# Loading the keys of a decode attention in 64 KB runs, on five slots used from both ends in turn

## The chip, the cores and the metric

The kernel runs on one core of one Trainium2 chip. The metric is the device time of one execution in microseconds (us). The profile is one execution of the same program under the hardware profiler. Its span begins with the first instruction of the program and is about 1.8 us shorter than the time.

## The reference

One new token for a batch of two passes two branches which a gate mixes: a small MLP mixer, and attention over a long cache. Only the attention matters here, because it reads nearly all the bytes.

```python
B, Sq, D = 2, 1, 1024
H, Sk, Dh = 32, 16384, 128          # k_cache, v_cache: (B, H, Sk, Dh) in bfloat16, 268 MB each
q = (x @ wq).reshape(B, Sq, H, Dh).transpose(0, 2, 1, 3)
scores = einsum("bhqd,bhkd->bhqk", q, k_cache) * Dh ** -0.5
p = softmax(scores, axis=-1)
o = einsum("bhqk,bhkd->bhqd", p, v_cache)
a = o.transpose(0, 2, 1, 3).reshape(B, Sq, H * Dh) @ wo
out = g * a + (1 - g) * b           # b: the MLP branch, g: a sigmoid gate
```

## The kernel before

The 64 pairs of batch and head are processed in 32 *couples* of two heads. A partition holds 256 consecutive positions of one head, which are 64 KB in one run in HBM. In the on-chip memory a ring of four slots of 32 KB per partition takes all large loads. The values of a couple take slots 0 and 1 in one load. The keys come as two loads of one slot each, so in runs of 32 KB.

```python
NRS = 4
SLOT = J * Dh                                    # 32 KB a partition
k_slots = (3, 2)
def q_k(n):                                      # keys of couple n: two loads
    for t in range(2):
        queue_load(("k", n, t), [lambda e, idx, t=t: e.dma_start(ring[:, idx, :],
                   kv_src(A_k, n)[:, t * SLOT:(t + 1) * SLOT])], (k_slots[t],))
def q_v(n):                                      # values of couple n: one load
    queue_load(("v", n), [lambda e, idx: e.dma_start(ring[:, idx:idx + 2, :].rearrange("p s m -> p (s m)"),
                                                     kv_src(A_v, n))], (0, 1))
# ... cut: all loads are queued in the order K0 V0 K1 V1 ..., and each is issued, in this order,
#     by the sync engine as soon as the last reader of its slots has signalled.

for n in range(NPR):                             # 32 couples; a hardware loop on TensorE, VectorE, ScalarE
    ev_z = do_Z(n)
    for c in range(NU // TC):                    # 8 chunks, 4 to a slot
        ev_t = do_T(n, c)                        # VectorE transposes a chunk of keys in place
        for t in range(TC):
            do_S(n, c * TC + t, ...)             # TensorE: scores; the slot is released after its 4th chunk
    ev_pt, ev_rc = do_softmax(n)
    ev_OT = do_out(n, do_PV(n, ev_pt), ev_rc)    # TensorE: probabilities times values; releases slots 0 and 1
# ... cut: at the end do_aproj multiplies with Wo, which comes in one load of 4 MB and six smaller pieces.
```

Of the kernel before, what the change touches and what calls it, by code (L numbers as in the profile page):

```python
# [7 lines left out]
ALU = mybir.AluOpType  # L8
AX = mybir.AxisListType
BF16 = mybir.dt.bfloat16  # L10
F32 = mybir.dt.float32
# [109 lines left out]
def build_kernel(nc, A_x, A_k, A_v, A_wq, A_wo, B_w1, B_w2, B_w3, B_w4, gate_w, out, dbg=None):  # L121
    dbg = dbg or {}
    B, Sq, D = A_x.shape
    _, H, Sk, Dh = A_k.shape
# [3 lines left out]
    P = 128  # L128
    J = Sk // P
    assert J == P  # L130
    HP = 2
    NU = 16
    JU = HP * J // NU
    UH = NU // HP
    NBP = 4
    G = B * H
    NPR = G // HP
    assert H % HP == 0
    NBD = D // P
    NBF = F // P  # L140
    NRS = 4
    SLOT = J * Dh
    NCOL = JU * 32
    ZO = 2 * (NU - 1)
# [17 lines left out]
    with ExitStack() as st:  # L162
        block = st.enter_context(nc.Block())
        sb = lambda name, shape, dt: st.enter_context(nc.sbuf_tensor(name, shape, dt))
        ring = sb("ring", [P, NRS, SLOT], BF16)
        ident = sb("ident", [P, P], BF16)
# [24 lines left out]
        recip = sb("recip", [P, HP], F32)  # L191
        OT_sb = sb("OT_sb", [P, G], BF16)
        rA = sb("rA", [P, 1], F32)
        hsel = sb("hsel", [P, HP, P], F32)
        gTt = sb("gTt", [P, NPR // B, B], F32)
        OT4_sb = sb("OT4_sb", [P, R4, NCT, 2], BF16)
        xrow = sb("xrow", [P, DQ], BF16)
        bgrow = sb("bgrow", [P, DQ], F32)
# [17 lines left out]
        gT = sb("gT", [P, 4], F32)  # L216
# [3 lines left out]
        esems = {e: sem("e_" + e) for e in ENGS}  # L220
        s_ring = [sem(f"dr{i}") for i in range(NRS)]
        s_misc = sem("dmisc")
# [4 lines left out]
        pl = _Plan(esems)  # L227
# [33 lines left out]
        for hp in range(HP):  # L261
# [7 lines left out]
                    waits=(ev_rowm,), sig=True)  # L269
# [3 lines left out]
                        waits=(e0,), sig=True)  # L273
# [3 lines left out]
        slot_of = {}  # L277
        slots_of = {}
        slot_free = {i: () for i in range(NRS)}

# [6 lines left out]
        def queue_load(key, fns, slots):  # L287
            dma_q.append((key, fns, slots))
# [9 lines left out]
                    dma_done[key] = dma_done[key, k] = pl.dma("sp", (lambda e, fn=fn, idx=slots[0]: fn(e, idx)), dsem,  # L298
                                                              waits=waits if k == 0 else ())

        def release(key, ev):
            for idx in slots_of[key]:
                assert idx not in slot_free
                slot_free[idx] = tuple(ev) if isinstance(ev, (tuple, list)) else (ev,)
            pump()

        def arrived(key):
            assert key in dma_done, f"load {key} not yet issued in program order (would deadlock)"
            return dma_done[key]
# [17 lines left out]
        wloads = {}  # L327
# [20 lines left out]



        w_slots = [0, 1, 2, 3, 0, 1, 2]
        k_slots = (3, 2)
        n_w = [0]

        def q_load(key):
# [3 lines left out]
        def kv_src(T, n):  # L359
            h, b = n // B * HP, n % B  # L360
            return T[b, h:h + HP].rearrange("h (p j) d -> (h p) (j d)", p=P // HP)

        def q_k(n):
            for t in range(2):
                queue_load(("k", n, t), [lambda e, idx, t=t: e.dma_start(ring[:, idx, :], kv_src(A_k, n)[:, t * SLOT:(t + 1) * SLOT])],
                           (k_slots[t],))

        def q_v(n):
            queue_load(("v", n), [lambda e, idx: e.dma_start(ring[:, idx:idx + 2, :].rearrange("p s m -> p (s m)"), kv_src(A_v, n))],
# [13 lines left out]
        evd = {}  # L383
# [13 lines left out]
        def rd5w():  # L397
            return (b5_lw[0],) + tuple(b5_rd)

        def rd5(ev):  # L400
            b5_rd.append(ev)
            return ev
# [5 lines left out]
        def st_gate():  # L408
            e1 = pl.add("dve", lambda e: e.tensor_tensor(zz[:, 0, :, :], xT_f[:, :, :],
                                                         gwT_f[:, :].unsqueeze(2).broadcast_to([P, NBD, 2]), op=ALU.mult),  # L410
                        waits=(evd["xT_f"], evd["gwT"]), sig=True)
            e2 = pl.add("dve", lambda e: e.tensor_reduce(gin[:, 0:2], zz[:, 0, :, :].rearrange("p n b -> p b n"), axis=AX.X, op=ALU.add),
                        waits=(e1,), sig=True)
            e3 = mm5(g_ps, ones_f[:, :], gin[:, 0:2], waits=(e2, ev_const), sig=True)
            e4 = rd5(pl.add("act", lambda e: e.activation(th[:, 0:2], g_ps, ACT.Tanh, scale=0.5), waits=(e3,) + rd5w(), sig=True))
            pl.add("dve", lambda e: e.tensor_scalar(gT[:, 0:2], th[:, 0:2], 0.5, 0.5, op0=ALU.mult, op1=ALU.add),
                   waits=(e4,), sig=True)
            evd["g"] = pl.add("dve", lambda e: e.tensor_scalar(gT[:, 2:4], th[:, 0:2], -0.5, 0.5, op0=ALU.mult, op1=ALU.add),
                              waits=(e4,), sig=True)
            evd["gTt"] = pl.add("dve", lambda e: e.tensor_copy(gTt[:, :, :], gT[:, 0:2].unsqueeze(1).broadcast_to([P, NPR // B, B])),  # L420
                                waits=(evd["g"],), sig=True)
            e5 = pl.add("dve", lambda e: e.tensor_tensor(gm[:, :], gT[:, 2:4], m2[:, :], op=ALU.mult),
                        waits=(evd["g"], ev_const), sig=True)
            evd["grow"] = pl.add("dve", lambda e: e.tensor_reduce(grow[:, :], gm[:, :], axis=AX.X, op=ALU.add), waits=(e5,), sig=True)
# [126 lines left out]
        key = ("w2", 0)  # L551
# [3 lines left out]
        for hi in range(NHI):  # L555
            key = ("w3", hi)
# [3 lines left out]
        for pi, (k0, kn) in enumerate(w4_parts):  # L560
            key = ("w4", pi)
            put([row_stage(key, list(range(c * R4, (c + 1) * R4)), k0 * R4, kn * R4, lambda kc: GT_bf[:, kc, :], "GT",
                               last=(c == kn - 1)) for c in range(kn)], key)
# [5 lines left out]
        for qd in range(NQ):  # L569
            ev_xr = pl.dma("act", lambda e, qd=qd: e.dma_start(xrow[32 * qd:32 * qd + 2, :], A_x[:, 0, qd * DQ:(qd + 1) * DQ]), s_xr,  # L570
                           waits=(ev_xr0,))
# [6 lines left out]
            q_k(n)  # L578
            q_v(n)
        for pi in range(2):  # L580
            queue_load(("wo", pi), wloads[("wo", pi)], (k_slots[pi],))
        pump()

        def xrow4(row, b_n, nb):
# [4 lines left out]
        last = None  # L589
        for nb in range(NBD):  # L590
            last = pl.add("pe", lambda e, nb=nb: e.transpose(tr_ps[:, nb * 4:nb * 4 + 2], xrow4(xg_row, 2, nb), ident[0:2, 0:2]),
                          waits=(ev_x, ev_ident), sig=(nb == NBD - 1))
# [8 lines left out]
        first = True  # L601
        ev = None
        for hi in range(NHI):
            key = ("wq", hi)
            ev_arr = arrived(key)
            wv = ring_w(slot_of[key], R4, HD)
            for r in range(R4):
                kc = hi * R4 + r
                for h in range(H):
# [4 lines left out]
                    ev = pl.add("pe", fn, waits=(ev_arr, ev_xT_bf) if h == 0 else (), sig=lastmm)  # L614
                    first = False
# [4 lines left out]
        for bp in range(NBP):  # L620
            evp = pl.add("pe", lambda e, bp=bp: e.matmul(q4_ps[:, bp, :], lhsT=PermQ[:, bp, :],  # L621
                                                        rhs=q_sb[:, :, :].rearrange("p h b -> p (h b)"), start=True, stop=True),
                         waits=(ev_q, ev_const, ev_r0), sig=(bp == NBP - 1))
# [3 lines left out]
        for nb in range(NBD):  # L627
            lastg = pl.add("pe", lambda e, nb=nb: e.transpose(gw_ps[:, nb, 0:1], xrow4(gw_row, 1, nb), ident[0:1, 0:1]),
                           waits=(ev_gw, ev_const), sig=(nb == NBD - 1))
        evd["gwT"] = pl.add("dve", lambda e: e.tensor_copy(gwT_f[:, :], gw_ps[:, :, 0]), waits=(lastg,), sig=True)  # L630
        pro_ev = (ev_q, ev_q4, evd["gwT"], evd["xT_f"], ev_xT_bf)
# [6 lines left out]
        oT_ps = banks[7][:, 0:HP]  # L638
        PH = P // HP
        TC = 2  # L640
# [10 lines left out]
                    waits=(ev_q4, ev_const, ev_S.get(n - 1)), sig=(hp == HP - 1))  # L651
            return ev

        def do_T(n, c):
            key, o = ("k", n, c * TC // UH), c * TC % UH * JU * Dh
            ap = ring[:, slot_of[key], o:o + TC * JU * Dh].bitcast(F32)
            return pl.add("dve", lambda e: e.transpose(ap, ap), waits=(arrived(key),), sig=True)  # L657

        def do_S(n, u, w):
            key, o = ("k", n, u // UH), u % UH * JU * Dh  # L660
            kv = ring[:, slot_of[key], o:o + JU * Dh].rearrange("p (j b k t) -> p j b k t", j=JU, b=2, k=32)
            end = u % UH == UH - 1
            for bp in range(NBP):
                ev = pl.add("pe", lambda e, bp=bp: e.matmul(  # L664
                    S_ps[:, 0:NCOL], lhsT=Z[:, bp, ZO - 2 * u:ZO - 2 * u + P], rhs=kv[:, :, bp // 2, :, bp % 2],
                    start=(u == 0 and bp == 0), stop=(u == NU - 1 and bp == NBP - 1), skip_group_check=True),
                    waits=w, sig=(end and bp == NBP - 1))
                w = ()
            if end:
                ev_S[n] = ev  # L670
                release(key, ev)

        def do_softmax(n):
            e1 = pl.add("dve", lambda e: e.tensor_reduce(rA[:, :], S_ps[:, 0:NCOL], axis=AX.X, op=ALU.max), waits=(ev_S[n],), sig=True)  # L674
# [33 lines left out]
        def do_out(n, ev_pv, ev_rc):  # L708
            e1 = pl.add("act", lambda e: e.activation(acc_sb[:, :], acc_ps[:, 0:512], ACT.Copy), waits=(ev_pv,), sig=True)  # L709
            for w in range(4):  # L710
                e2 = pl.add("pe", lambda e, w=w: e.matmul(oT_ps, lhsT=acc_sb[:, w * P:(w + 1) * P], rhs=dsel[:, w, :],  # L711
                                                          start=(w == 0), stop=(w == 3)), waits=(e1,) if w == 0 else (), sig=(w == 3))
            return pl.add("dve", lambda e, i: e.scalar_tensor_tensor(  # L713
                OT_sb[:, bass.ds(i * HP, HP)], oT_ps, gTt[:, :, :].rearrange("p m b -> p (m b)")[:, bass.ds(i, 1)], recip[:, :],
                op0=ALU.mult, op1=ALU.mult), waits=(e2, ev_rc), sig=True, dyn=True)

        def do_aproj():
            o4_ps = banks[7][:, 16:16 + R4 * NCT * 2].rearrange("p (r c b) -> p r c b", r=R4, b=2)
# [24 lines left out]
        for n in range(NPR):  # L743
            pl.mark[n] = {e: len(pl.ops[e]) for e in ENGS}
            ev_z = do_Z(n)
            for c in range(NU // TC):
                ev_t = do_T(n, c)
                for t in range(TC):
                    do_S(n, c * TC + t, () if t else (ev_t, ev_z) + (pro_ev if c == 0 else ()) if c == 0 else (ev_t,))
            ev_pt, ev_rc = do_softmax(n)  # L750
            ev_OT = do_out(n, do_PV(n, ev_pt), ev_rc)
        pl.mark[NPR] = {e: len(pl.ops[e]) for e in ENGS}
# [4 lines left out]
        for b, eng in enumerate(("sp", "act")):  # L757
            ev_out = pl.dma(eng, lambda e, b=b: e.dma_start(out[b, 0, :].rearrange("(q n) -> q n", q=NQ), orow[b:PR:32, :]), s_out[b],
                            waits=(ev_fin,))
            pl.add(eng, lambda e, ev=ev_out: e.wait_ge(ev.sem, ev.val))  # L760

        def loop_of(name):
            first = pl.mark[0][name]
            return first, pl.mark[1][name] - first, NPR

        @block.gpsimd
        def _(e):
# [64 lines left out]
```

## Time and profile before

| | before |
|---|---|
| time, median of 4 | 1329.43 us (1329.35 to 1329.55) |
| bytes read | 570.4 MB |
| packets of the load queue | 17,000 |
| from couple to couple (landings of values) | 38.780 us |
| last value landing, last Wo landing | 1304.43, 1324.41 us |

A packet is one run of bytes that one of the 16 DMA engines moves (or the 4 bytes with which it reports a load's end; they take their engine 6 ns in the packet records of before). The last row comes from the trace's landing records: a load leaves 16 records there, one for each DMA engine, and has landed with the last. These lines are from the page of before. The first two rows under the span give busy time and share by engine, the DMA row is the busy share of the DMA engines in 40 slices of the span, and the last rows are groups of instructions: busy time, mean ns of one, then the engine's idle time just before them and what ended it.

```profile
span 1327.6 us, 12590 instructions
...
PE 803.9 (61%) x5306; PEld 327.0 (25%) x5306; DVE 659.3 (50%) x521; ACT 45.7 (3%) x99; POOL 20.1 (2%) x101
...
DMA  9999999999999999999999999999999999999998
...
q1 hardware_dynamic: 17000, 570.43, 99.7%
q8 instruction: 8, 0.13, 0.0%
...
DMA 72%; DVE 16%; PE 6%; issue 6%; SPq 0%; ACT 0%
...
L657 DVE STREAM_TRANSPOSE ring<-ring 128x2048 f32<-128x2048 f32 x256 | 569.0, 2280 | 108.6 <-DMA ring<-in_A_k_cache_dram 108.6
...
L700 PE MATMUL ps<-ring,PT_sb 128*32 128x512 bf16 x2048 | 183.4, 537 | 152.7 <-DMA ring<-in_A_v_cache_dram 152.7
```

No compute engine is busy for more than 61% of the span, but the load queue q1 fills 99.7% of the 16 engines' time, and the DMA row stands at 90% or more in every slice but the last. Both the transposes of keys and the matmuls on values start when a DMA lands. q8: the 8 packets of 16 KB there are blocks of instructions.

One couple in the timeline of before (start, duration, engine, line, operation; in brackets the idle time before it and what ended it; SPq is the sync engine issuing a load):

```profile
606.43 6.00 PE L700 MATMUL ps<-ring,PT_sb 128*32 128x512 bf16 x64 [4.55 <-DMA ring<-in_A_v_cache_dram]
...
612.48 0.33 SPq L369 DMA_DIRECT2D ring<-in_A_v_cache_dram  x1
...
616.12 8.89 DVE L657 STREAM_TRANSPOSE ring<-ring 128x2048 f32<-128x2048 f32 x4 [2.26 <-DMA ring<-in_A_k_cache_dram]
...
625.84 8.89 DVE L657 STREAM_TRANSPOSE ring<-ring 128x2048 f32<-128x2048 f32 x4 [0.83 <-DMA ring<-in_A_k_cache_dram]
627.16 9.90 SPq L365 DMA_DIRECT2D ring<-in_A_k_cache_dram  x2
```

The first half of the keys lands at 616.1 us and the second at 625.8. The next keys are issued at 627.2, while the values are in flight until 645: every load is queued long before its predecessor ends.

### The profile page before, as it was taken

The page shows a single profiled execution, that of the slowest core. Times are in us where ns is not written, and L with a number is a line of the kernel's source. Part 1 is how long each engine was busy: PE and PEld are TensorE (multiplying, and loading weights), DVE is VectorE, ACT ScalarE, POOL GpSimd, SP SyncE. Part 2 cuts the span into 40 slices and gives each one's busy share as a digit, 9 for nine tenths or more (in the row PEclk, how much of TensorE's full clock was granted, in tenths as well). Part 3 has the DMA queues.
Part 4 walks back from the last instruction along what each step waited for, and adds up shares of the span by engine and source line. Part 5 has one row for each costly group of instructions (what it writes and reads, how often), then busy time and mean ns, then how long its engine had stood idle before and what let it go on. Part 6 is the DMA issues. An engine that isn't in the chain of part 4 may idle for free.

```text
span 1327.6 us, 12590 instructions
## 1 busy us (share of the span) xinstructions
PE 803.9 (61%) x5306; PEld 327.0 (25%) x5306; DVE 659.3 (50%) x521; ACT 45.7 (3%) x99; POOL 20.1 (2%) x101
## 2 busy tenths in 40 slices
PE   3456555766655566665557666555656655565764
PEld 3322221222222222222222222222222222222222
DVE  1065544466544456654445665444566544456650
ACT  0000000000000000000000000000000000000000
POOL 2000000000000000000000000000000000000000
PEclk9997778778877877887778787777888777788877
DMA  9999999999999999999999999999999999999998
GB/s 400 429 439 429 440 427 427 433 431 439 432 440 427 422 436 431 436 440 427 430 430 432 434 436 442 427 427 429 432 433 440 434 427 436 425 434 429 447 430 348
DMA packets 17041, 570.60 MB, mean 430 GB/s; under 512 B 1779, under 2 KB 1795, under 8 KB 2182
## 3 DMA queue, kind: packets, MB, share of 16 engines
q1 hardware_dynamic: 17000, 570.43, 99.7%
q8 instruction: 8, 0.13, 0.0%
q14 instruction: 3, 0.02, 0.0%
q10 hardware_dynamic: 30, 0.01, 0.0%
HBM read 570.44 MB, written 0.00 MB: 430 GB/s over the span
## 4 chain that ended last, share of the span: by engine, by line
DMA 72%; DVE 16%; PE 6%; issue 6%; SPq 0%; ACT 0%
DMA ring<-in_A_k_cache_dram 66%; DVE ring L657 16%; PE ps L664 5%; DMA ring<-in_B_w_dram 2%; DMA ring<-in_A_wo_dram 2%; DMA ring<-in_A_wq_dram 2%; SPq L324 0%; PE ps L514 0%; PE ps L612 0%; PE ps L485 0%; PE ps L405 0%; DVE orow L756 0%; DVE q_f L624 0%; PE ps L734 0%; PE ps L621 0%
## 5 line engine op out<-in xcount | busy, mean ns | idle before, releaser
L664 PE MATMUL ps<-ring,Z 128*128 128x512 bf16 x2048 | 540.0, 418 | 217.8 <-DVE ring L657 217.3
L657 DVE STREAM_TRANSPOSE ring<-ring 128x2048 f32<-128x2048 f32 x256 | 569.0, 2280 | 108.6 <-DMA ring<-in_A_k_cache_dram 108.6
L664 PEld LDWEIGHTS ps<-ring,Z 128*128 128x128 bf16 x2048 | 199.9, 104 | 545.1 <-issue 273.4
L700 PE MATMUL ps<-ring,PT_sb 128*32 128x512 bf16 x2048 | 183.4, 537 | 152.7 <-DMA ring<-in_A_v_cache_dram 152.7
L713 DVE SCALAR_TENSOR_TENSOR OT_sb<-ps,gTt,recip 128x2 f32 x32 | 7.0, 219 | 368.3 <-PE ps L711 368.3
L700 PEld LDWEIGHTS ps<-ring,PT_sb 128*32 128x32 bf16 x2048 | 67.6, 130 | 255.4 <-DMA ring<-in_A_v_cache_dram 155.4
L674 DVE TENSOR_REDUCE rA<-ps 128x1 f32<-128x512 f32 x32 | 22.1, 691 | 64.3 <-PE ps L664 64.3
L685 ACT ACTIVATE P_sb<-ps,negm 128x512 bf16<-128x512 f32 x32 | 22.0, 687 | 851.5 <-DVE negm L683 851.5
L689 PE MATMUL ps<-rowsum,hsel 128*128 128x1 f32 x128 | 23.8, 290 | 37.9 <-ACT P_sb L685 37.9
L687 DVE STREAM_TRANSPOSE PT_sb<-P_sb 128x512 bf16<-128x512 bf16 x32 | 22.8, 711 | 27.0 <-ACT P_sb L685 27.0
L709 ACT ACTIVATE acc_sb<-ps 128x512 bf16<-128x512 f32 x32 | 19.1, 597 | 363.4 <-PE ps L700 363.4
L689 PEld LDWEIGHTS ps<-rowsum,hsel 128*128 128x128 f32 x128 | 21.1, 234 | 40.7 <-ACT P_sb L685 40.7
L647 POOL TENSOR_TENSOR Z<-q_f,mask 128x8 bf16<-128x8 f32 x64 | 12.3, 226 | 1208.2 <-PE ps L664 1208.2
L676 PE MATMUL ps<-ident,rmax_bf 128*1 128x128 bf16 x32 | 7.0, 217 | 33.1 <-DVE rmax_bf L675 33.1
L711 PE MATMUL ps<-dsel,acc_sb 128*128 128x2 bf16 x128 | 8.1, 167 | 22.7 <-ACT acc_sb L709 22.7
L612 PE MATMUL ps<-xT_bf,ring 128*128 128x2 bf16 x256 | 7.1, 165 | 17.8 <-DMA ring<-in_A_wq_dram 17.8
L711 PEld LDWEIGHTS ps<-dsel,acc_sb 128*128 128x128 bf16 x128 | 5.3, 96 | 38.4 <-ACT acc_sb L709 38.4
L676 PEld LDWEIGHTS ps<-ident,rmax_bf 128*1 128x1 bf16 x32 | 2.5, 79 | 49.1 <-DVE rmax_bf L675 49.1
L677 DVE TENSOR_REDUCE m_sb<-ps 1x2 bf16<-1x128 bf16 x32 | 8.9, 279 | 9.9 <-PE ps L676 9.9
L683 DVE TENSOR_SCALAR negm<-ps,cAB 128x1 f32<-128x1 f32 x32 | 8.8, 276 | 9.2 <-PE ps L680 9.2
L680 PE MATMUL ps<-m_sb,ones_bf 1*64 1x1 bf16 x64 | 6.1, 186 | 11.9 <-DVE m_sb L677 11.9
L514 PE MATMUL ps<-ring,GT_bf 128*2 128x256 bf16 x112 | 6.3, 415 | 10.1 <-DMA ring<-in_B_w_dram 10.1
(93 smaller groups left out, 91.0 us busy)
## 6 DMA issues: line engine op xcount, KB each, us to landing
ring<-in_A_k_cache_dram SPq DMA_DIRECT2D x64, 4096.0 KB, 27.8
ring<-in_A_wq_dram SPq DMA_DIRECT2D x2, 4096.0 KB, 17.5
ring<-in_B_w_dram SPq DMA_DIRECT2D x2, 3584.0 KB, 32.3
ring<-in_B_w_dram SPq DMA_DIRECT2D x1, 4096.0 KB, 28.5
ring<-in_A_wo_dram SPq DMA_DIRECT2D x1, 4096.0 KB, 26.5
ring<-in_B_w_dram SPq DMA_DIRECT2D x1, 3072.0 KB, 29.1
ring<-in_A_wo_dram SPq DMA_DIRECT2D x3, 1024.0 KB, 23.0
ring<-in_B_w_dram SPq DMA_DIRECT2D x1, 2048.0 KB, 27.3
```

The source lines that it names most:

```text
L647: ev = pl.add("pool", lambda e, hp=hp: e.tensor_tensor(Z[:, :, ZO:ZO + P].rearrange("p t (i c) -> p t i c", c=32)[:, :, 2 * hp:2 * hp + 2, ...
L657: return pl.add("dve", lambda e: e.transpose(ap, ap), waits=(arrived(key),), sig=True)
L664: ev = pl.add("pe", lambda e, bp=bp: e.matmul(S_ps[:, 0:NCOL], lhsT=Z[:, bp, ZO - 2 * u:ZO - 2 * u + P], rhs=kv[:, :, bp // 2, :, bp % 2], ...
L674: e1 = pl.add("dve", lambda e: e.tensor_reduce(rA[:, :], S_ps[:, 0:NCOL], axis=AX.X, op=ALU.max), waits=(ev_S[n],), sig=True)
L676: e3 = pl.add("pe", lambda e: e.transpose(mt_ps, rmax_bf[:, :], ident[:, :]), waits=(e2,), sig=True)
L677: e4 = pl.add("dve", lambda e: e.tensor_reduce(m_sb[0:1, :], mt_ps.rearrange("o (h p) -> o h p", h=HP), axis=AX.X, op=ALU.max), waits=(e3, ...
L685: e7 = pl.add("act", lambda e: e.activation(P_sb[:, :], S_ps[:, 0:NCOL], ACT.Exp, bias=negm[:, 0:1], scale=scale, accum_out=rowsum[:, 0:1] ...
L687: e8 = pl.add("dve", lambda e: e.transpose(PT_sb[:, :], P_sb[:, :]), waits=(e7,), sig=True)
L689: e9 = pl.add("pe", lambda e, hp=hp: e.matmul(l_ps[:, hp:hp + 1], lhsT=hsel[:, hp, :], rhs=rowsum[:, 0:1], start=True, stop=True, skip_gro ...
L700: ev = pl.add("pe", lambda e, jj=jj, cg=cg: e.matmul(acc_ps[32 * cg:32 * cg + 32, 0:512], lhsT=PT_sb[:, 32 * jj:32 * jj + 32], rhs=vv[:, 4 ...
L709: e1 = pl.add("act", lambda e: e.activation(acc_sb[:, :], acc_ps[:, 0:512], ACT.Copy), waits=(ev_pv,), sig=True)
L711: e2 = pl.add("pe", lambda e, w=w: e.matmul(oT_ps, lhsT=acc_sb[:, w * P:(w + 1) * P], rhs=dsel[:, w, :], start=(w == 0), stop=(w == 3)), w ...
```

## The change

Keys are to come in 64 KB runs as the values do, one load a couple. A fifth slot would not hold a second pair, so couples take turns: even ones lie in slots 3 and 4 and are processed from the lower half, odd ones in slots 2 and 3, from the upper half. In either case slot 3 is processed first, and its release together with the slot that is free already lets the next keys be issued. The hardware loop now spans two couples and runs 16 rounds.

```diff
-    NRS = 4
+    NRS = 5
 ...
-        w_slots = [0, 1, 2, 3, 0, 1, 2]
-        k_slots = (3, 2)
+        w_slots = [0, 1, 2, 3, 4, 0, 1]
+        k_slots = ((3, 4), (2, 3))
+        k_order = ((0, 1), (1, 0))
 ...
-            for t in range(2):
-                queue_load(("k", n, t), [lambda e, idx, t=t: e.dma_start(ring[:, idx, :], kv_src(A_k, n)[:, t * SLOT:(t + 1) * SLOT])],
-                           (k_slots[t],))
+            queue_load(("k", n), [lambda e, idx: e.dma_start(ring[:, idx:idx + 2, :].rearrange("p s m -> p (s m)"), kv_src(A_k, n))],
+                       k_slots[n % 2])
 ...  (do_T, do_S: take their chunk from the two slots; do_S releases one slot of the two after each half;
 ...   a small table gTt gives way to the gate itself, now that the batch index is fixed within the loop body)
-            queue_load(("wo", pi), wloads[("wo", pi)], (k_slots[pi],))
+            queue_load(("wo", pi), wloads[("wo", pi)], ((4, 3)[pi],))
 ...
-            for c in range(NU // TC):
-                ev_t = do_T(n, c)
+            us = [h * UH + v for h in k_order[n % 2] for v in range(UH)]
+            for k in range(0, NU, TC):
+                ev_t = do_T(n, us[k])
 ...
-            return first, pl.mark[1][name] - first, NPR
+            return first, pl.mark[2][name] - first, NPR // 2
```

More of the change, by code (lines that the diff above doesn't have):

```diff
@@ L194, in build_kernel @@
         hsel = sb("hsel", [P, HP, P], F32)
-        gTt = sb("gTt", [P, NPR // B, B], F32)
         OT4_sb = sb("OT4_sb", [P, R4, NCT, 2], BF16)
@@ L299, in pump, with release @@
                                                               waits=waits if k == 0 else ())
-        def release(key, ev):
-            for idx in slots_of[key]:
+        def release(key, ev, slots=None):
+            for idx in slots or slots_of[key]:
                 assert idx not in slot_free
@@ L419, in st_gate @@
                               waits=(e4,), sig=True)
-            evd["gTt"] = pl.add("dve", lambda e: e.tensor_copy(gTt[:, :, :], gT[:, 0:2].unsqueeze(1).broadcast_to([P, NPR // B, B])),
-                                waits=(evd["g"],), sig=True)
             e5 = pl.add("dve", lambda e: e.tensor_tensor(gm[:, :], gT[:, 2:4], m2[:, :], op=ALU.mult),
@@ L652, in do_Z, with chunk, do_T, do_S @@
             return ev
-        def do_T(n, c):
-            key, o = ("k", n, c * TC // UH), c * TC % UH * JU * Dh
-            ap = ring[:, slot_of[key], o:o + TC * JU * Dh].bitcast(F32)
-            return pl.add("dve", lambda e: e.transpose(ap, ap), waits=(arrived(key),), sig=True)
-        def do_S(n, u, w):
-            key, o = ("k", n, u // UH), u % UH * JU * Dh
-            kv = ring[:, slot_of[key], o:o + JU * Dh].rearrange("p (j b k t) -> p j b k t", j=JU, b=2, k=32)
+        def chunk(n, u, nu):
+            o = u * JU * Dh
+            return ring[:, slot_of["k", n]:slot_of["k", n] + 2, :].rearrange("p s m -> p (s m)")[:, o:o + nu * JU * Dh]
+        def do_T(n, u):
+            ap = chunk(n, u, TC).bitcast(F32)
+            return pl.add("dve", lambda e: e.transpose(ap, ap), waits=(arrived(("k", n)),), sig=True)
+        def do_S(n, u, w, first, last):
+            kv = chunk(n, u, 1).rearrange("p (j b k t) -> p j b k t", j=JU, b=2, k=32)
             end = u % UH == UH - 1
@@ L665, in do_S @@
                     S_ps[:, 0:NCOL], lhsT=Z[:, bp, ZO - 2 * u:ZO - 2 * u + P], rhs=kv[:, :, bp // 2, :, bp % 2],
-                    start=(u == 0 and bp == 0), stop=(u == NU - 1 and bp == NBP - 1), skip_group_check=True),
+                    start=(first and bp == 0), stop=(last and bp == NBP - 1), skip_group_check=True),
                     waits=w, sig=(end and bp == NBP - 1))
@@ L670, in do_S @@
                 ev_S[n] = ev
-                release(key, ev)
+                release(("k", n), ev, (slots_of["k", n][u // UH],))
         def do_softmax(n):
@@ L712, in do_out @@
                                                           start=(w == 0), stop=(w == 3)), waits=(e1,) if w == 0 else (), sig=(w == 3))
+            b = n % B
             return pl.add("dve", lambda e, i: e.scalar_tensor_tensor(
-                OT_sb[:, bass.ds(i * HP, HP)], oT_ps, gTt[:, :, :].rearrange("p m b -> p (m b)")[:, bass.ds(i, 1)], recip[:, :],
-                op0=ALU.mult, op1=ALU.mult), waits=(e2, ev_rc), sig=True, dyn=True)
+                OT_sb[:, bass.ds(i * B * HP + b * HP, HP)], oT_ps, gT[:, b:b + 1], recip[:, :], op0=ALU.mult, op1=ALU.mult),
+                waits=(e2, ev_rc), sig=True, dyn=True)
         def do_aproj():
@@ L745, in build_kernel @@
             ev_z = do_Z(n)
-            for c in range(NU // TC):
-                ev_t = do_T(n, c)
+            us = [h * UH + v for h in k_order[n % 2] for v in range(UH)]
+            for k in range(0, NU, TC):
+                ev_t = do_T(n, us[k])
                 for t in range(TC):
-                    do_S(n, c * TC + t, () if t else (ev_t, ev_z) + (pro_ev if c == 0 else ()) if c == 0 else (ev_t,))
+                    w = () if t else (ev_t,) if k else (ev_t, ev_z) + pro_ev
+                    do_S(n, us[k + t], w, k + t == 0, k + t == NU - 1)
             ev_pt, ev_rc = do_softmax(n)
```

## The prediction

> **What bounds the kernel now.** The DMA engines. The page gives 570.6 MB in 1327.6 us, with the load queue's packets filling 99.7% of the 16 engines' span. By the packet records the engines idle about 5.5 us in the mean, 3.7 us of it behind the last weight load. In the chain of waits the DMA has 72%; the DVE transposes in it (16%) only stand there because a key load's issue waits for its slot, far ahead of need. Landings of couples are 38.78 us apart: two key loads of 4 MB at 9.712 us each, a value load of 8 MB at 19.354 us: 16.78 MB at 432.7 GB/s. [...]
>
> **What the change removes.** Keys come in 64 KB runs, as values do. A 64 KB packet takes its engine 2.419 us, a 32 KB packet about 1.214 us, so joining two saves some 9 ns; one completion descriptor (6 ns) per load and engine goes too. By landings: 2 x 9.712 - 19.354 = 0.070 us a couple, x 32 = 2.2 us, all on the critical path, as the queue is never empty. The gTt copy was not critical.
>
> **What it adds and moves.** Work on keys begins only when all 8 MB have landed, one half (9.7 us) later. With T this landing:
> - The first half is scored about T + 12 (now 10.95 to 12.6 us from landing to the issue its release allows); then the next keys are issued. The fastest engines finish the values ahead of them about T + 17.5: margin 5 us; from an issue to its first packet passes about 1 us.
> - The second half follows without pause (eight transposes of 2.27 us, 18 us); softmax is done near T + 23.5 (14.6 us from a half's landing to transposed probabilities). Values landed at T + 19.4, so PV now waits 4 us for softmax, not for the DMA. It takes 5 to 6 us; the next values are issued near T + 30, the queue runs dry only at T + 37: margin 7 us.
> - Prologue: the first values still wait for the last W4 matmuls (66.7 us), with keys in flight until about 81.
> - Tail: Wo loads are issued no later than needed; the last PV ends about 4 us later, near the landing of the first Wo load, and its last pieces still come after. Ending unchanged.
> - The loop body doubles, 16 rounds. Instruction loads are 8 packets of 16 KB in the whole run; I expect no more inside the loop.
>
> So 1329.5 - 2.2 = **1327.3 us**, eight times in ten between 1326.4 and 1328.4. Faster by over 2%: 1%. Within 2%: 96%. Slower by over 2%: 3%.
>
> **What would show it.** Landings of couples 38.71 us apart; the load queue's 17,000 packets fewer by some 4,600, key packets 64 KB at 2.42 us; engine idle not over 6 us; the wait ahead of PV's first matmul ends with the transposed probabilities, not the values; DVE waits for keys once a couple, 10 to 15 us.
>
> **What would make it wrong.** An issue too late: were the TensorE clock halved (now 7 to 10 us after each pause) over a whole first half, scoring it would take 16 us and the key margin fall to 1 us; starvation would show as engine idle time once a couple. Or instruction reloads in the longer loop that burden one DMA engine.

For the 16 us at half clock: in the trace of before the granted clock falls to 0.5 in 65 stretches, 63 of which last 6.8 or 10.2 us (601.0 to 611.3 and 614.7 to 621.5 us in the couple above). In the second of them a matmul on keys came every 0.43 us, so 32 of them and the first transpose would take 16 us, by estimate.

## The result, and the profile after

The changed kernel takes 1328.49 us (median of 4, 1328.13 to 1328.50) against 1329.43 us. The ratio is 0.9992 with a 95% interval of 0.9975 to 1.0009. A ratio here is the mean time of one kernel's fast runs over that of the other's fast runs of the same rounds, so not quite the ratio of the medians quoted. By this interval alone the two are the same; the eight single times do not overlap, however, and the trace shows where the 0.9 us comes from.

The page of after:

```profile
span 1326.7 us, 12413 instructions
...
PE 778.5 (59%) x5306; PEld 329.5 (25%) x5306; DVE 655.4 (49%) x520; ACT 45.7 (3%) x99; POOL 20.1 (2%) x101
...
DMA  9999999999999999999999999999999999999998
...
q1 hardware_dynamic: 12392, 570.43, 99.6%
q8 instruction: 9, 0.15, 0.0%
...
DMA 71%; PE 22%; DVE 6%; SPq 1%; issue 0%
...
L658 DVE STREAM_TRANSPOSE ring<-ring 128x2048 f32<-128x2048 f32 x256 | 565.2, 2275 | 278.6 <-DMA ring<-in_A_k_cache_dram 278.6
...
L700 PE MATMUL ps<-ring,PT_sb 128*32 128x512 bf16 x2048 | 169.6, 505 | 4.5 <-DVE recip L691 4.5
```

The same bytes come in 4,608 packets fewer. The matmuls on values (L700) no longer wait for a DMA: the idle time before them fell from 152.7 to 4.5 us, as softmax is now what comes last. In the chain of waits the DMA keeps its 71%; that TensorE's matmuls now stand there for the transposes means only that they release the slot for the next keys, far ahead of need. One couple in the timeline of after:

```profile
586.12 17.66 DVE L658 STREAM_TRANSPOSE ring<-ring 128x2048 f32<-128x2048 f32 x8 [8.50 <-DMA ring<-in_A_k_cache_dram]
...
597.20 0.33 SPq L365 DMA_DIRECT2D ring<-in_A_k_cache_dram  x1
...
609.68 6.50 PE L700 MATMUL ps<-ring,PT_sb 128*32 128x512 bf16 x64
...
616.24 0.33 SPq L369 DMA_DIRECT2D ring<-in_A_v_cache_dram  x1
```

All eight transposes run without a pause from the landing at T = 586.1. The next keys are issued at T + 11.1, the matmuls on values start at T + 23.6, and the next values are issued at T + 30.1. The queue still never runs dry: over all couples, keys are issued at least 4.8 us before the fastest engine has finished the load ahead of them, and values at least 6.3 us.

The landing records of the two traces, us from the start of the span:

| | before | after | gained so far |
|---|---|---|---|
| values of the first couple | 102.27 | 102.33 | -0.06 |
| values of the last couple | 1304.43 | 1302.07 | 2.36 |
| last Wo piece but one | 1323.76 | 1321.44 | 2.32 |
| last Wo piece | 1324.41 | 1323.51 | 0.90 |
| end of the span | 1327.61 | 1326.68 | 0.93 |

So the couples gained what was expected: (1304.43 - 102.27) / 31 = 38.780 us each before, 38.701 after, 0.078 us a couple. But 1.4 us was given back in the last of 78 landings. The end of before:

```profile
1321.87 1.02 PE L734 MATMUL ps<-ring,OT_sb 128*2 128x256 bf16 x16 [1.87 <-DMA ring<-in_A_wo_dram]
1323.14 1.04 PE L734 MATMUL ps<-ring,OT_sb 128*2 128x256 bf16 x12 [0.25 <-DMA ring<-in_A_wo_dram]
1324.45 0.38 PE L734 MATMUL ps<-ring,OT_sb 128*2 128x256 bf16 x4 [0.27 <-DMA ring<-in_A_wo_dram]
```

and of after:

```profile
1320.79 0.39 PE L735 MATMUL ps<-ring,OT_sb 128*2 128x256 bf16 x8 [0.65 <-DMA ring<-in_A_wo_dram]
1321.49 0.28 PE L735 MATMUL ps<-ring,OT_sb 128*2 128x256 bf16 x4 [0.30 <-DMA ring<-in_A_wo_dram]
1323.55 0.28 PE L735 MATMUL ps<-ring,OT_sb 128*2 128x256 bf16 x4 [1.78 <-DMA ring<-in_A_wo_dram]
```

The last four matmuls waited 1.78 us for their piece of Wo where before they waited 0.27. In the packet records one of the 16 engines pauses in after from 1320.97 to 1322.04 us, with seven packets of 2 KB of that last piece to go: the time of a q8 packet of 16 KB, 1320.97 to 1322.05. This is a block of TensorE's instructions: u_pad7 and u_pad9 below have 1,792 and 2,304 TensorE instructions more, nothing else, and q8 has 7 and 9 packets more, one for 256 instructions. The engine's next three packets take 0.23 us each for the usual 0.084. It was the engine furthest behind: the others had at most four packets to go. Before loads a block at its end as well, the eighth, at 1322.96 us, but there no packet of a load is delayed: the engine that this block took had ended its share of Wo.

**Theory.** Two things make the result. First, the gain is the larger packets' alone. Second, instruction blocks take turns over some of the DMA engines, each holds its engine for about 1.5 us (in after 1.07 us of pause and some 0.45 us on the packets behind it), and since all engines are full to the end (99.6% of the span), the engine that had most blocks ends last. The doubled loop body makes TensorE's program longer (2,330 instructions for 2,037), which is one block more, and it fell on an engine that had been held before, while the eighth block of before fell on one that was ahead. **Rivals:** the gain comes from the fifth slot and the order of the halves; the difference is noise; the late last piece comes from the new slots or issue order of Wo.

### The profile page after: what moved, and what is told of

Read it like the earlier page. It is cut to its first block, busy times and chain, and to the rows that moved or that the text cites. A ratio compares the mean times of both kernels' runs of the same rounds, so it can differ in the third digit from the quotient of the medians.

```text
span 1326.7 us, 12413 instructions
## 1 busy us (share of the span) xinstructions
PE 778.5 (59%) x5306; PEld 329.5 (25%) x5306; DVE 655.4 (49%) x520; ACT 45.7 (3%) x99; POOL 20.1 (2%) x101
## 3 DMA queue, kind: packets, MB, share of 16 engines
q1 hardware_dynamic: 12392, 570.43, 99.6%
## 4 chain that ended last, share of the span: by engine, by line
DMA 71%; PE 22%; DVE 6%; SPq 1%; issue 0%
DMA ring<-in_A_k_cache_dram 66%; PE ps L664 22%; DVE ring L658 6%; DMA ring<-in_B_w_dram 3%; DMA ring<-in_A_wo_dram 2%; SPq L323 0%; PE ps L483 0%; SPq L314 0%; DVE orow L759 0%; PE ps L735 0%
## 5 line engine op out<-in xcount | busy, mean ns | idle before, releaser
L664 PE MATMUL ps<-ring,Z 128*128 128x512 bf16 x2048 | 530.7, 416 | 393.0 <-DVE ring L658 392.3
L658 DVE STREAM_TRANSPOSE ring<-ring 128x2048 f32<-128x2048 f32 x256 | 565.2, 2275 | 278.6 <-DMA ring<-in_A_k_cache_dram 278.6
L700 PE MATMUL ps<-ring,PT_sb 128*32 128x512 bf16 x2048 | 169.6, 505 | 4.5 <-DVE recip L691 4.5
L714 DVE SCALAR_TENSOR_TENSOR OT_sb<-ps,gT,recip 128x2 f32 x32 | 7.0, 220 | 205.3 <-PE ps L711 205.3
L700 PEld LDWEIGHTS ps<-ring,PT_sb 128*32 128x32 bf16 x2048 | 68.6, 123 | 91.7 <-issue 71.3
L512 PE MATMUL ps<-ring,GT_bf 128*2 128x256 bf16 x112 | 6.0, 402 | 10.2 <-DMA ring<-in_B_w_dram 10.2
```

The source lines that it names most:

```text
L658: return pl.add("dve", lambda e: e.transpose(ap, ap), waits=(arrived(("k", n)),), sig=True)
L664: ev = pl.add("pe", lambda e, bp=bp: e.matmul(S_ps[:, 0:NCOL], lhsT=Z[:, bp, ZO - 2 * u:ZO - 2 * u + P], rhs=kv[:, :, bp // 2, :, bp % 2], ...
L700: ev = pl.add("pe", lambda e, jj=jj, cg=cg: e.matmul(acc_ps[32 * cg:32 * cg + 32, 0:512], lhsT=PT_sb[:, 32 * jj:32 * jj + 32], rhs=vv[:, 4 ...
```

## The experiments

Both kernels wait, within their hardware loop, on semaphores against register values. All variants have the loop written out, with constant waits. That makes TensorE's program 10,695 instructions long and brings some 41 instruction blocks for 8 or 9. They are compared with one another in the same rounds, not with the looped kernels.

```diff
-            return pl.add("dve", lambda e, i: e.scalar_tensor_tensor(
+            return pl.add("dve", lambda e, i=n // B: e.scalar_tensor_tensor(
 ...  (this is u_after; u_before has i=n)
-            pl.emit("pe", e, loop_of("pe"))
+            pl.emit("pe", e)                      # likewise for dve and act
```

### 1. u_before and u_after: both kernels written out

> The kernel before with its loop over the 32 couples written out, so that every semaphore wait is against a constant; nothing else differs. It is the base of the written-out variants. Theory (the DMA engines are full and only what their packets take counts): couples still 38.78 us apart up to the cost of more instruction loads; TensorE's instruction blocks of 16 KB rise from 8 to about 42, each holds one DMA engine about 1 us, some 2 more an engine: 1331.5 us, between 1329.5 and 1334. Rival (instruction loads cost nothing): 1329.4.

> The changed kernel with the loop written out. Theory (64 KB packets save 0.07 us a couple, and the last Wo landing was late only because an instruction block met it on one engine): last value landing 2.4 us ahead of u_before's, whole time 1 to 3 us less, depending on where the last instruction block falls. Rival (the gain of 0.9 us in the first comparison was noise): no difference in the landings.

Measured: u_before 1336.75 us (5 runs, 1336.54 to 1337.25), u_after 1334.56 us (1334.40 to 1335.98). The change gains 2.2 us in this form, and the last value landing came 2.7 us earlier (1310.77 and 1308.08). From the first couple's value landing to the last couple's it is 1208.43 us in u_before and 1206.00 in u_after, 2.43 us less, the same difference as between the looped kernels (1202.17 and 1199.74). The 0.9 us of the first comparison was therefore not noise around zero.

Writing the loop out cost more than I expected: 7.2 us for before (1329.53 us in the same rounds), where 2 were expected. The landings say why. The 16 engines' landings of the last couple's values in u_before, in us after the first of them:

```
0.00 0.02 0.07 0.14 0.58 0.60 0.69 4.24 | 7.75 7.84 7.85 7.88 7.93 7.98 8.16 8.17
```

Eight engines are about 8 us behind the early ones, in place of the 1.9 us of the looped kernel. I had spread the blocks over 16 engines. They fall on eight: 33 more blocks are about four more on each, and writing out lengthened the way from the first to the last value landing by 6.26 us in both kernels (1208.43 - 1202.17, and 1206.00 - 1199.74), so about 1.56 us a block. The packet records agree: 1.07 us of pause, and the packet after it about 0.5 us longer. They also show the turns: in u_before the blocks' own times repeat with a period of eight (the 11th and 12th, the 19th and 20th, and so on up to the 36th take 1.02 to 1.03 us, all others from the seventh on 1.06 or more). Writing out also raised q14's instruction blocks of 8 KB from 3 to 7. Four of them took about 1 us each of what seems to be one engine, which fits the lone 4.24 in the list.

The gap between the two groups is not always 8 us. In u_after it is 4.4, because the early eight were slowed too: between 110 and 1290 us, 39 of its key and value packets that do not follow an instruction block took over 0.2 us longer than usual, in clusters at the borders of loads. In u_before no packet did but the 38 that follow a block. What slows these early engines was not looked for. They do not set the time.

### 2. u_k32: the new slots and order, the old packets

```diff
-            queue_load(("k", n), [lambda e, idx: e.dma_start(ring[:, idx:idx + 2, :].rearrange("p s m -> p (s m)"), kv_src(A_k, n))],
+            queue_load(("k", n), [lambda e, idx, t=t: e.dma_start(ring[:, idx + t, :], kv_src(A_k, n)[:, t * SLOT:(t + 1) * SLOT]) for t in range(2)],
```

(With it, both parts count on the slot's one semaphore, and its full count is awaited.)

> u_after with each couple's keys as two loads of 32 KB runs, issued one after the other into the same two slots and waited for together: slots, turn-taking and order of work stay those of the change, only the packets go back to 32 KB. Theory (packet size is the gain): couples 38.78 us apart again, 2.2 to 2.6 us slower than u_after. Rival (the fifth slot or the order of the halves is the gain): as u_after.

Measured: 1337.27 us (1336.95 to 1337.84), 2.7 us slower than u_after in the same rounds, and as slow as u_before. From the first to the last value landing it takes 1208.37 us, as u_before does (1208.43). Everything of the change but the one load of 64 KB runs is still there, and the gain is gone. The fifth slot and the order of the halves gain nothing by themselves. That it is the packets and not the second load a couple, u_k32 alone cannot tell; u_k8 can.

### 3. u_k8: a larger dose

```diff
+            queue_load(("k", n), [lambda e, idx, t=t: e.dma_start(
+                ring[:, idx:idx + 2, :].rearrange("p s m -> p (s m)").rearrange("p (a t m) -> p t a m", t=2, m=4096)[:, t],
+                kv_src(A_k, n).rearrange("p (a t m) -> p t a m", t=2, m=4096)[:, t]) for t in range(2)], k_slots[n % 2])
```

> u_after with each couple's keys in 8 KB runs (two loads, every second run each). Theory (a fixed cost of 8 to 9 ns a packet): an 8 KB packet takes about 310.5 ns, so eight of them take 65 ns more than one of 64 KB; 8 rows an engine and couple, 0.52 us a couple, 16.5 us in all: about 1.2% slower than u_after. Rival (runs over a few KB are all alike, the step from 32 to 64 KB is only the load's own overhead): no more than 1 us slower than u_k32.

Measured: 1351.47 us (1350.95 to 1352.22), 16.9 us slower than u_after for 16.5 expected. From its page:

```profile
span 1349.7 us, 11594 instructions
...
q1 hardware_dynamic: 41576, 570.43, 99.8%
```

An engine's step from packet to packet is 310.8 ns at 8 KB, 1,214 ns at 32 KB and 2,419 ns at 64 KB. From 8 to 64 KB that is 2,108 ns for 56 KB, 37.65 ns a KB, which leaves 310.8 - 301.2 = 9.6 ns for the packet itself. The same line gives 1,214.4 ns at 32 KB. So a packet costs some 9 to 10 ns at each of these three sizes, and the rival that all long runs are alike is out by a factor of more than ten.

### 4. u_after2, u_pad7, u_pad9: more instruction blocks

Tiny matmuls into an unused bank are put after each couple, where TensorE pauses for 7 us and more (11.0 us before the keys' first matmul at 632.1 us in u_pad9). They change nothing but the length of its program; 36 of them take 1.05 us.

```diff
             ev_OT = do_out(n, do_PV(n, ev_pt), ev_rc)
+            for _ in range(7 * 256 // 2 // NPR):   # u_pad9: 9 * 256; a matmul is two instructions
+                pl.add("pe", lambda e: e.matmul(banks[4][0:32, 0:2], lhsT=ident[:, 0:32], rhs=ident[:, 0:2], start=True, stop=True))
```

> The written-out changed kernel once more, unchanged, as the base in the same rounds as the three below: 1334.6 us, within 0.6.

> u_after with 7 x 256 more TensorE instructions (28 tiny matmuls into an unused bank after each couple, in the pause of 7 us before the next keys land), so seven more instruction blocks of 16 KB. Theory (blocks go to 8 of the 16 DMA engines in turn, each holds its engine 1.5 us, and the slowest engine alone sets the time; 41 loads before the end are five on each of eight and a sixth on one): 48 loads are six on each of eight, so the slowest engine is unchanged: 0, within 0.5 us, of u_after2. Rival (each further block costs its share): 7 x 1.5 / 8 = 1.3 us slower.

> As u_pad7 with nine more blocks: 50 loads. Theory: two engines get a seventh, so 1.5 us slower than u_after2 and than u_pad7. Rival (proportional): 1.7 us slower than u_after2, but only 0.4 slower than u_pad7.

Measured: u_after2 1334.65 us (1334.35 to 1335.45), u_pad7 1334.90 (1334.67 to 1335.46), u_pad9 1336.18 (1335.89 to 1337.40). Seven more blocks cost 0.25 us, within the scatter; nine cost 1.5 us. A cost in proportion would have given 1.3 and 1.7. It goes in steps, as the theory says: the blocks are dealt out in turn and the fullest engine counts.

### 5. u_nq2: one block less

```diff
-    NQ = 4
+    NQ = 2
```

> u_after with the matmuls of the row products (W2, W4, Wo) twice as wide, 512 columns in two column groups for 256 in four: 136 matmuls and 272 TensorE instructions fewer, so one block fewer, 40 before the end. Theory: the engine with a sixth block is gone, the last Wo landing comes 1.4 us earlier relative to the last value landing, about 1.4 us faster than u_after2. Rival (the last landing's delay comes from the slots or the order of the Wo loads, not from instruction blocks): its last landing as late as u_after2's, the time at most 0.3 us less for the shorter last matmuls.

Measured: 1333.49 us (1333.35 to 1333.74), 1.16 us faster than u_after2, with no overlap of their runs. It is correct. The time from the last value landing to the last Wo landing is 19.89 us against 21.43 in u_after2. The Wo slots and the order of the loads are the same in both. In the timeline of u_after2 the last matmuls come at

```profile
1328.34 1.03 PE L735 MATMUL ps<-ring,OT_sb 128*2 128x256 bf16 x12 [0.65 <-DMA ring<-in_A_wo_dram]
1329.61 0.38 PE L735 MATMUL ps<-ring,OT_sb 128*2 128x256 bf16 x4 [0.24 <-DMA ring<-in_A_wo_dram]
```

and in u_nq2 at

```profile
1326.83 1.04 PE L735 MATMUL ps<-ring,OT_sb 128*2 128x512 bf16 x6 [0.21 <-DMA ring<-in_A_wo_dram]
1328.12 0.38 PE L735 MATMUL ps<-ring,OT_sb 128*2 128x512 bf16 x2 [0.25 <-DMA ring<-in_A_wo_dram]
```

The last matmuls themselves take as long as before (0.38 us), so the gain is the landing. The 16 engines' landings of the last piece of Wo, the latest nine of them, in us after the first:

```
u_before  4.14 7.61 7.69 7.71 7.76 7.79 7.82 7.98 9.58     41 blocks, old slots
u_after2  1.01 3.69 3.72 3.82 3.82 3.86 3.88 3.94 5.64     41 blocks
u_nq2     2.20 3.75 3.89 3.90 4.11 4.17 4.23 4.28 4.37     40 blocks
u_pad7    0.88 4.32 4.50 4.54 4.60 4.68 4.74 4.76 4.90     48 blocks
u_pad9    1.31 3.24 3.33 3.38 3.39 4.04 4.07 5.02 5.68     50 blocks
after     1.08 1.36 1.41 1.53 1.57 1.60 1.66 1.69 3.38      9 blocks, looped
before    1.29 1.45 1.57 1.61 1.63 1.67 1.68 1.82 1.88      8 blocks, looped
```

With a multiple of eight blocks (40, 48) a group of eight ends together; in before, nine engines do, its eighth block having delayed no load. With one more (41, and 9 in after) one engine stands 1.6 to 1.7 us behind that group; with two more (50) two stand 1.0 and 1.6 us behind. This is what the theory says of after. The row of u_before answers the last rival: with the slots and the issue order of before, but 41 blocks, one engine is late too, and its last Wo landing comes 21.41 us after the last value landing (19.97 in before, 19.88 in u_pad7, which has the new slots).

### 6. u_fixed: without taking turns

```diff
-        k_slots = ((3, 4), (2, 3))
-        k_order = ((0, 1), (1, 0))
+        k_slots = ((3, 4), (3, 4))
+        k_order = ((0, 1), (0, 1))
```

> u_after with the turn-taking taken out: every couple's keys lie in the slots 3 and 4 and are processed from the lower half, so the next keys can be issued only after both halves are scored. The packets, the number of loads and the fifth slot stay. Theory (the queue stays full only because the issue comes ahead of the fastest engine's end of the values, 17.4 us after the keys' landing): scoring ends 19.7 us after the landing, the first packet follows about 1 us later, at T + 20.7, when all engines have run dry; the next landing comes 19.4 us after that, so a couple takes 40.2 to 40.6 us for 38.9, some 40 to 50 us in all: 1375 us, between 1365 and 1390, with engine idle time in every couple. Rival (64 KB runs alone carry the gain and the order of the halves does not matter): as u_after, 1334.6.

Measured: 1444.27 us (4 runs, 1443.18 to 1445.77), 8.6% slower than before by the ratio (1.0859) and some 110 us more than u_after (another chip). A couple takes 42.45 us, so 3.55 us more than in u_after; I had expected 1.3 to 1.7. In stretches of 4 us (busy time by engine, granted clock, DMA share, GB/s) it looks so:

```profile
604.00:608.00 4.00, 4.00 (x20) 1.63 (x17) 4.00 (x3) 0.00 (x0) 0.00 (x0) 1.00 1.21 524
608.00:612.00 4.00, 3.72 (x17) 1.38 (x16) 2.23 (x2) 0.00 (x0) 0.00 (x0) 1.00 0.05 16
612.00:616.00 4.00, 1.27 (x12) 0.76 (x15) 2.29 (x6) 0.78 (x2) 0.38 (x2) 1.00 0.79 262
```

A packet is counted in the stretch in which it starts, hence shares over 1; the 0.05 is the gap. The keys landed at 592.5 us. The engines ended the values from 609.4 us on, most of them before 610, T + 17. The next keys were issued at 612.23, T + 19.7 as expected, but the first packets followed at 613.2 and took 2.8 to 3.4 us each for the usual 2.42.

The issue and the first packet came when they were expected, at T + 19.69 and T + 20.65 in the mean of 30 couples. What was too small is the time from there to the next landing, 21.7 us for 19.4. The median engine takes 20.5: its first packet after the pause takes 3.1 us, and the landing is reported some 0.5 us after its last. The last engine comes 1.2 us later still, and an instruction block is why. About one block comes in a couple: in the 20 couples where one came after the keys' issue, the last engine was 1.3 to 2.0 us behind the median, and in nine of the ten others 0.2 to 0.5 (in the tenth, where the block came just before the issue, 1.2). So with an empty queue, which lines the engines up at each couple, nearly every block costs time, and not only the last one of eight.

## Why the prediction was right or wrong

- **Right.** It foresaw no difference of 2%. The runs allow this estimate: before has 12,288 key and value packets, 768 on each engine, and at the 9.6 ns a packet of u_k8 they cost 7.4 us, 0.6% of the time. If the time for each KB stays as in these runs, re-cutting these loads cannot save much more. From couple to couple the rate was 432.6 GB/s before and 433.5 after (16.78 MB in 38.701 us).
- **The mechanism was right, and so was its size.** "2 x 9.712 - 19.354 = 0.070 us a couple, x 32 = 2.2 us": measured 0.078 us a couple and 2.36 us at the last value landing. u_k32 and u_k8 show that packets alone make it.
- **The margins were right.** Expected: the next keys at T + 12, PV (the matmuls on values) at T + 23.5, the next values near T + 30, margins of 5 and 7 us. Medians measured: 11.7, 23.5, 28.8, margins of 5.6 and 7.8. u_fixed shows that they are needed.
- **"Ending unchanged" is the step that failed.** It was out by 1.47 us: from the last value landing to the last Wo landing 19.97 us before, 21.44 after. With it the time is 1328.5, 1.2 us over the central value and at the upper edge of the range (0.09 us above it). I had named instruction reloads as a risk of the loop, and expected none there because 8 blocks in the whole run seemed nothing. (Inside the loop one more came than before: three in after, from 102.2 to 150.9 us, and two in before, at 93.0 and 1004.0 us. After 150.9 us the longer body ran without a block until 1321.0.) In fact the load of one block more at the very end, on one engine, took back 60% of the gain. The steps of the padded kernels, u_nq2, and u_before with the old slots show it for the written-out kernels; in the looped kernel itself it is inferred from the packet and landing records, because no variant of it could be run.
- **Two signs were misjudged.** "Engine idle not over 6 us": it was 6.8 up to the last DMA packet, of which 5.2 lie behind the last Wo load (3.7 in before): the 15 other engines wait for the late one. "DVE waits for keys once a couple, 10 to 15 us": once it was, but 278.6 / 32 = 8.7 us, since VectorE's small steps for softmax and output lie in between.
- **Left open.** u_nq2 points to a version that should beat both kernels: the changed kernel in its loop, with the row products twice as wide. Its program would be about 272 instructions shorter, some 2,058, which is ten more than eight blocks of 256 (the number from u_pad7 and u_pad9); if that saves a block, I estimate 1.2 to 1.4 us from the step seen written out. It was not run. Written out, the best version (1333.5 us) is slower than both looped kernels.

## What to carry to other kernels

When the DMA engines are full, count what each packet and each load costs (here 9 to 10 ns, and 6 ns an engine), and expect no more than that sum from recutting loads; here 4,096 packets fewer on keys were worth 0.2%. A queue is full only if each load is issued before the *fastest* engine ends the one ahead of it (in the couple of u_fixed shown above the issue came 2.8 us after that, and a couple took 3.55 us more), so find the slot whose release comes too late and reorder the work to release it first. And in such a kernel the program is traffic as well: a longer instruction stream lengthens the run by what it adds to the slowest DMA engine (7.2 us for 33 blocks more in u_before), so compare landings engine by engine and keep hot loops rolled up.
